# A two-stage kernel with a hand-written order: operand loads and sums moved within a pass, the first step on five banks, low parts and tile copies moved within a step

## The chip, the cores and the metric

The kernel runs on one core of one Trainium2 chip. The metric is the device time of one execution in microseconds (us). Times below are from three unprofiled runs and one profiled execution of the kernel before.

## The reference

Two stages. The first is a complex linear recurrence with an outer-product state, for 4 batches and 8 heads, 768 positions and head size 48; its output y, read as 3072 tokens of width 384, goes into a mixture of 8 experts whose gate P is normalised over rows and columns eight times.

```python
for t in range(S):
    S_re, S_im = a_re*S_re - a_im*S_im + outer(k[t], v[t]), a_re*S_im + a_im*S_re
    y[t] = q[t] @ S_re
x = y as (3072, 384)
P = exp(x @ w_gate - max);  8 times: P /= P.sum(1); P /= P.sum(0); P *= N / E
out = sum over e of P[:, e] * (relu(x @ w1[e]) @ w2[e])      # w1: 384 x 1024, w2: 1024 x 384
```

## The kernel before

Every float32 product is made of three matmuls on two rounded parts (hi x hi, hi x lo, lo x hi), so each operand exists as a high and a low part.

**Phase 1** (about the first 600 us) runs the recurrence in blocks of 256 tokens and, beside it, experts 0 and 1 (`experts`, L193). Their results go by the tile `yst` (L211 to L213) to the tensors ye_d in memory. The Sinkhorn normalisation starts at its end (`phase2a`): `rows` on VectorE, then `columns`, which begins with a small matmul on the sum cs; between them `more(3)` sends three groups of expert work to TensorE (L919 to L930).

**Phase 2** (`phase2b`) runs experts 2 to 7. The tokens are cut into 4 passes (u = 0 to 3) of 768. A pass has 16 steps (m), a step three hidden blocks of 128; I count the steps through, n = 16u + m. Odd passes go through the weights backwards. A step has two kinds of work on TensorE, interleaved by hand:

- 15 products P1 to P15 (`prod`) of sums of weight blocks with sums of token blocks, a scheme of Strassen's kind which takes 15 block products for 18. A product is three matmuls of 384 columns into a PSUM bank. The banks are X and Y, where Z and V take over Y's and P takes over X's. After a product, ACT copies the bank into a tile (`copy`: 11, 12, 21, 31, 32) or VectorE adds it to one (`add`); only then may the next product write the bank. Finished tiles become hh (high part, ACT) and hl (low part, VectorE), the hidden activations; hl00, hl10 and so on name block and token half.
- 18 units (`unit`) of the step before: three matmuls each, from hh and hl into an output bank `po`. When an expert is complete, `finish` (L986) accumulates po, scaled by P, in oa.

`fill(s)`, for slots s = 0 to 14, stands between the products: it issues one or two units, the jobs that `todo` has for this slot, one or two `xjobs`, and a finish. VectorE, ACT and SP take their instructions in this written order. Each is in order, so an instruction that waits holds up all that stand behind it.

Beside this run, by SP's queue: in passes 1 to 3 the weight set of the next step (`load_set`: wa, wb, wc, wd, 768 KB each), in slot 0; in the last step of a pass the 15 operands of the next (`swap`, xP). In passes 1 and 2 the operands of the pass after the next step are made (`forms_late`): eight copies within memory (plain, xf<-x_d), loads of the parts of x (xb, xt), their sums (`full`, L743), and for each form a high part by ACT (stP, L755), a low part by VectorE (L760) and a store (xf). The six y tiles of pass 0 and of the own pass, the results of experts 0 and 1, are loaded by `early` (L961) and added into the result by VectorE (L973); for pass 0 the result is loaded from od, where pass 0 left it, and stored to the output (L975). y, od and stP share the three buffers of the pool `st`.

Of the kernel before, what the change touches and what calls it, by code (L numbers as in the profile page):

```python
# [72 lines left out]
class Net:  # L73
# [122 lines left out]
    def experts(self):  # L196
# [3 lines left out]
        def l2(i, e, f, hh, hl):  # L200
            w2h = self.wt[e, f][:, 0, C:]
            w2l = self.wt[e, f][:, 1, C:]
            for k in range(NCH):
                if f == 0:
                    po[k] = self.psB.tile([128, C], F32, tag="po", name=f"po{e}_{i}_{k}")
                s = slice(k * 128, k * 128 + 128)
                nc.tensor.matmul(po[k], hh[:, s], w2h, start=f == 0, stop=False)  # L207
                nc.tensor.matmul(po[k], hh[:, s], w2l, start=False, stop=False)  # L208
                nc.tensor.matmul(po[k], hl[:, s], w2h, start=False, stop=f == NF - 1)  # L209
                if f == NF - 1:  # L210
                    st = self.xp.tile([128, C], F32, tag="yst", name=f"yst{e}_{i}_{k}")  # L211
                    nc.scalar.activation(st, po[k], AF.Copy)  # L212
                    nc.sync.dma_start(self.ye_d[e][i * NCH + k], st)  # L213
# [677 lines left out]
    def phase2a(self, c2):  # L891
# [30 lines left out]
        for k in range(HEAD):  # L922
            self.rows()
            more(3)
# [9 lines left out]
    def phase2b(self, c2):  # L934
# [89 lines left out]
        xjobs = []  # L1024
        for n, (u, t) in enumerate(steps):
# [21 lines left out]
            if u == 0 and m == 6:  # L1047
                for k in (3, 4, 5, 0, 1, 2):
                    rescale(0, k)
            for uu, ms in ((0, (1, 2, 4, 5, 12, 13)), (u, (6, 7, 8, 9, 10, 11))):  # L1050
                if u and m in ms and (uu or u == 1):
                    y = []
                    todo.setdefault(1, []).append(lambda uu=uu, k=ms.index(m), y=y: y.append(early(uu, k)))
                    todo.setdefault(7, []).append(lambda y=y: y[0]())
# [38 lines left out]
            def fill(s):  # L1093
# [5 lines left out]
                if u and s in (1, 3, 5) and 0 < m < NT - 1 and xjobs:  # L1099
# [3 lines left out]
                if u and m == 0 and s == 14 and xjobs:  # L1103
                    for _ in range(3):
                        xjobs.pop(0)()
                if s < 8 or s in (10, 11, 12):
                    if fin:
                        fin.pop(0)[1]()

            if u and m == 0:  # L1110
                for _ in range(FRONT):
                    unit(*units.pop(0))
            prod("P1", "X", True)
# [44 lines left out]
            l00()  # L1158
# [4 lines left out]
            l10()  # L1163
# [6 lines left out]
            l21()  # L1170
            carry.append(hh(2, 0, c["31"]))
# [184 lines left out]
```

## Time and profile before

| | us |
|---|---|
| median of three runs | 1796.05 (1795.58 to 1797.16) |
| profiled execution | 1798.53 |
| its span, first to last instruction | 1796.8 |
| TensorE busy | 1728.0 |
| VectorE busy | 1270.7 |
| ACT busy | 738.6 |

PE is TensorE's matmul, PEld its weight load, DVE is VectorE, SPq the sequencer that issues transfers. A row of a timeline has the start in us, the duration, the engine, the line, the output and input tiles, and in brackets the idle time ahead of it with what ended it. A row of the list of waits has the total, the count and the longest. Phase 2 begins at 648.2 us of the span; its steps follow each other at about 17 us. A matmul is booked for 0.33 us and starts 0.17 us after the one before, since they are pipelined; the granted clock, PEclk, is 1.00 at full speed.

### The profile page before, as it was taken

The numbers are of one execution on the slowest core, as the hardware profiler recorded it, in microseconds if no ns is written. First come the engines' busy times: TensorE is split into PE (matmuls) and PEld (weight loads), VectorE is DVE, ScalarE is ACT, GpSimd is POOL, SyncE is SP. The second block draws the span as 40 slices with busy tenths as digits, with TensorE's granted clock in tenths as the row PEclk, the third lists the DMA queues.
The fourth block names the chain that finished last, engine by engine and source line by source line (L and its number), as shares of the span: only waits on it lengthen the run. The fifth ranks groups of instructions, "written<-read, shape, count | busy, mean of one in ns | idle before, by whom it ended". The sixth has DMA issues, their size and how long they took to land.

```text
span 1796.8 us, 31293 instructions
## 1 busy us (share of the span) xinstructions
PE 1728.0 (96%) x11774; PEld 1683.8 (94%) x11774; DVE 1270.7 (71%) x2710; ACT 738.6 (41%) x1673; POOL 191.7 (11%) x360
## 2 busy tenths in 40 slices
PE   6989999999999989999997999998999999999998
PEld 4988899999999989999997999997999999999998
DVE  7888999898897668877754566654566655556554
ACT  7544454554544545544522433332433333333231
POOL 3101111111111223334200000000000000000000
PEclk9989999999999999999999999998999999999999
DMA  6434444534357865667558766666666655556550
GB/s 214 115 99 125 109 118 121 155 116 116 110 150 261 324 251 221 255 230 283 203 181 270 254 235 221 231 213 215 228 221 220 222 192 197 200 193 209 191 208 29
DMA packets 160832, 346.04 MB, mean 193 GB/s; under 512 B 15264, under 2 KB 101536, under 8 KB 160672
## 3 DMA queue, kind: packets, MB, share of 16 engines
q1 hardware_dynamic: 155264, 334.03, 54.4%
q0 software_dynamic: 4608, 9.52, 2.2%
q8 instruction: 95, 1.56, 0.3%
q14 instruction: 65, 0.53, 0.1%
q10 hardware_dynamic: 800, 0.39, 0.1%
HBM read 232.53 MB, written 98.70 MB: 184 GB/s over the span
## 4 chain that ended last, share of the span: by engine, by line
PE 79%; DVE 12%; DMA 4%; ACT 2%; issue 2%; SPq 1%; DVEq 0%; ACTq 0%
PE po L1020 10%; PE po L1018 10%; PE po L1019 10%; PE ph L234 8%; PE X L1069 4%; PE X L1071 3%; PE X L1070 3%; PE po L207 3%; PE po L209 3%; PE po L208 3%; PE Y L1069 2%; PE Y L1071 2%; PE Y L1070 2%; PE sp L577 2%; DMA xt<-x_d 2%
## 5 line engine op out<-in xcount | busy, mean ns | idle before, releaser
L1020 PE MATMUL po<-wd,hl 128*128 128x384 f32 x768 | 257.3, 335 | 0.0
L1019 PE MATMUL po<-wd,hh 128*128 128x384 f32 x768 | 257.0, 335 | 0.0
L1018 PE MATMUL po<-wd,hh 128*128 128x384 f32 x768 | 256.9, 335 | 0.0
L234 PE MATMUL ph<-xh,w 128*128 128x256 f32 x1152 | 227.9, 283 | 2.1 <-ACT xh L646 1.2
L234 PEld LDWEIGHTS ph<-xh,w 128*128 128x128 f32 x1152 | 187.1, 191 | 3.1 <-ACT xh L646 1.8
L246 ACT ACTIVATE hh<-ph 128x256 fp32r<-128x256 f32 x192 | 73.3, 382 | 201.2 <-PE ph L234 200.6
L234 PE MATMUL ph<-xl,w 128*128 128x256 f32 x576 | 154.8, 283 | 0.5 <-DVE xl L647 0.5
L1020 PEld LDWEIGHTS po<-wd,hl 128*128 128x128 f32 x768 | 144.4, 188 | 0.8 <-DVE hl L1091 0.2
L1018 PEld LDWEIGHTS po<-wd,hh 128*128 128x128 f32 x768 | 144.5, 188 | 0.0
L1019 PEld LDWEIGHTS po<-wd,hh 128*128 128x128 f32 x768 | 144.5, 188 | 0.0
L207 PE MATMUL po<-w,hh 128*128 128x384 f32 x384 | 140.9, 367 | 2.5 <-ACT yst L212 2.4
L209 PE MATMUL po<-w,hl 128*128 128x384 f32 x384 | 130.7, 340 | 2.6 <-DVE hl L248 2.6
L208 PE MATMUL po<-w,hh 128*128 128x384 f32 x384 | 129.8, 338 | 0.0
L1020 PE MATMUL po<-wc,hl 128*128 128x384 f32 x384 | 128.7, 335 | 0.0
L1018 PE MATMUL po<-wc,hh 128*128 128x384 f32 x384 | 128.7, 335 | 0.0
L1019 PE MATMUL po<-wc,hh 128*128 128x384 f32 x384 | 128.7, 335 | 0.0
L539 POOL DMA_DIRECT2D qs<-z x144 | 77.2, 543 | 444.7 <-ACT hf L247 81.2
L234 PEld LDWEIGHTS ph<-xl,w 128*128 128x128 f32 x576 | 106.5, 190 | 0.9 <-DVE xl L647 0.9
L1090 ACT ACTIVATE hh<-X 128x384 fp32r<-128x384 f32 x64 | 31.5, 492 | 183.4 <-PE X L1071 183.4
L248 DVE TENSOR_TENSOR hl<-hf,hh 128x256 fp32r<-128x256 f32 x192 | 81.7, 427 | 27.6 <-ACT hf L247 26.3
L1001 DVE SCALAR_TENSOR_TENSOR oa<-po,P,oa 128x384 f32<-128x384 f32 x120 | 73.2, 614 | 21.1 <-PE po L1020 20.9
L207 PEld LDWEIGHTS po<-w,hh 128*128 128x128 f32 x384 | 73.1, 190 | 8.0 <-issue 4.0
(1822 smaller groups left out, 4400.2 us busy)
## 6 DMA issues: line engine op xcount, KB each, us to landing
wd<-wd SPq DMA_DIRECT2D x58, 768.0 KB, 6.0
wa<-wd SPq DMA_DIRECT2D x42, 768.0 KB, 4.4
wb<-wd SPq DMA_DIRECT2D x42, 768.0 KB, 5.7
wc<-wd SPq DMA_DIRECT2D x42, 768.0 KB, 4.5
xP<-xf SPq DMA_DIRECT2D x60, 384.0 KB, 4.5
raw<-in_w_dram SPq DMA_DIRECT2D x12, 1152.0 KB, 7.7
wd<-wc SPq DMA_DIRECT2D x16, 768.0 KB, 4.0
wd<-wa SPq DMA_DIRECT2D x16, 768.0 KB, 4.1
```

Of the source, the lines that this page charges most:

```text
L207: nc.tensor.matmul(po[k], hh[:, s], w2h, start=f == 0, stop=False)
L208: nc.tensor.matmul(po[k], hh[:, s], w2l, start=False, stop=False)
L209: nc.tensor.matmul(po[k], hl[:, s], w2h, start=False, stop=f == NF - 1)
L234: nc.tensor.matmul(ph, w[:, k, ct * 128:ct * 128 + 128], x[:, ct, :], start=q == 0, stop=q == len(terms) - 1)
L248: nc.vector.tensor_tensor(hl, hf, hh.bitcast(F32), ALU.subtract)
L539: dma = eng.dma_start(dst[q:q + D - 2:NCT, :, :w], src[:, a, ct * NCH + c, :w])
L1018: nc.tensor.matmul(po[k], hh[:, s], w2[0], start=c == 1, stop=False)
L1019: nc.tensor.matmul(po[k], hh[:, s], w2[1], start=False, stop=False)
L1020: nc.tensor.matmul(po[k], hl[:, s], w2[0], start=False, stop=c == NF)
L1069: nc.tensor.matmul(ps, w[:, 0, k], x[:, 0], start=start, stop=False, skip_group_check=True)
L1070: nc.tensor.matmul(ps, w[:, 0, k], x[:, 1], start=False, stop=False, skip_group_check=True)
L1071: nc.tensor.matmul(ps, w[:, 1, k], x[:, 0], start=False, stop=True, skip_group_check=True)
```

## The change

Seven edits, all in the written order; no instruction is added or dropped.

1. **Loads and sums of the next operands.** In step m = 0 the copies go to slot 4 and the first loads to slots 8 and 9 (all three were in slot 14); in the steps behind it the jobs run in slots 3, 5 and 7 (they were in 1, 3 and 5).
2. **The y tiles** are loaded in slot 2 (before: 1), and summed in slot 1 of the next step (before: slot 7 of the same).
3. **The first step** (n = 0), which has no units between its products, has an order of its own. Z, V and P have banks of their own there, so it uses five banks.
4. **Last low parts:** the add of bank V into 32 stands ahead of hl00, and hl10 behind hl21.
5. **Tile copies:** `finish` may run in slots 9, 10, 11 in place of 10, 11, 12.
6. **yst** of the last block lies in the pool st, which stays, not in the pool of phase 1.
7. **Column sums:** 4, 3 and 2 groups between rows and columns, not 3, 3 and 3.

```diff
-                    st = self.xp.tile([128, C], F32, tag="yst", name=f"yst{e}_{i}_{k}")
+                    if i == self.N // SUB - 1:
+                        st = self.st.tile([128, 2, C], F32R, tag="st", name=f"yst{e}_{i}_{k}").bitcast(F32)[:, 0]
+                    else:
+                        st = self.xp.tile([128, C], F32, tag="yst", name=f"yst{e}_{i}_{k}")
...
-            more(3)
+            more(4 - k)
...
+            todo.setdefault(1, []).extend(late)
+            late = []
             for uu, ms in ((0, (1, 2, 4, 5, 12, 13)), (u, (6, 7, 8, 9, 10, 11))):
                 if u and m in ms and (uu or u == 1):
                     y = []
-                    todo.setdefault(1, []).append(lambda uu=uu, k=ms.index(m), y=y: y.append(early(uu, k)))
-                    todo.setdefault(7, []).append(lambda y=y: y[0]())
+                    todo.setdefault(2, []).append(lambda uu=uu, k=ms.index(m), y=y: y.append(early(uu, k)))
+                    late.append(lambda y=y: y[0]())
...
-                if u and s in (1, 3, 5) and 0 < m < NT - 1 and xjobs:
+                if u and s in (3, 5, 7) and 0 < m < NT - 1 and xjobs:
...
-                if u and m == 0 and s == 14 and xjobs:
-                    for _ in range(3):
-                        xjobs.pop(0)()
-                if s < 8 or s in (10, 11, 12):
-                    if fin:
-                        fin.pop(0)[1]()
+                if u and m == 0 and s in (4, 8, 9) and xjobs:
+                    xjobs.pop(0)()
+                if fin and (s < 8 or s in (9, 10, 11)):
+                    fin.pop(0)[1]()
...
+            if n == 0:
+                prod("P1", "X", True)
+                copy("12", "X")
+                prod("P2", "Y", True)
+                copy("11", "Y")
+                prod("P3", "Z", True)
+                copy("21", "Z")
+                copy("31", "Z")
+                fill(0)
+                prod("P4", "X")
+                add("11", "X")
+                prod("P10", "Y")
+                add("31", "Y")
+                prod("P15", "V", True)
+                copy("32", "V")
+                prod("P7", "X")
+                add("21", "X")
+                prod("P5", "Z")
+                add("11", "Z")
+                l00 = hh(0, 0, c["11"])()
+                prod("P8", "Y")
+                add("32", "Y")
+                prod("P13", "X")
+                add("31", "X")
+                prod("P9", "Y")
+                add("12", "Y")
+                l01 = hh(0, 1, c["12"])()
+                prod("P14", "V")
+                add("31", "V")
+                prod("P11", "X")
+                add("32", "X")
+                l01()
+                l21 = hh(2, 1, c["32"])()
+                prod("P6", "P", True)
+                add("21", "P")
+                l10 = hh(1, 0, c["21"])()
+                prod("P12", "X")
+                hh(1, 1, bank["X"])()()
+                l21()
+                l00()
+                l10()
+                carry.append(hh(2, 0, c["31"]))
+                for k in range(1, 15):
+                    fill(k)
+                continue
...
             add("21", "P")
-            l00()
             l10 = hh(1, 0, c["21"])()
             fill(12)
             prod("P15", "V", True)
             add("32", "V")
-            l10()
+            l00()
             l21 = hh(2, 1, c["32"])()
...
             l21()
+            l10()
```

Three places of the written order, as built. First **SP's queue at the start of pass 1** (step 16 into step 17). od are the stores of pass 0's result, xf2<-x_d2 the eight copies, xb2 and xt2 the loads of x, wa13 to wd13 the next weight set. Before:

```order
L1003 DMA od3_166<-oa_0_9462 128x384
L1003 DMA od4_167<-oa_0_9462 128x384
L1003 DMA od5_168<-oa_0_9462 128x384
L1003 DMA od0_163<-oa_0_9462 128x384
L767 DMA xf2_161<-x_d2_93 128x3x128 x8
L739 DMA xb2_11869<-x_d2_93 128x3x128
L739 DMA xt2_1_12034<-x_d2_93 128x3x128
L739 DMA xb2_11869<-x_d2_93 128x3x128
L739 DMA xt2_2_12037<-x_d2_93 128x3x128
L861 DMA wa13_64_12050<-wd13_156 128x1536
L861 DMA wb13_65_12052<-wd13_156 128x1536
```

Now, from just behind the store od3:

```order
L770 DMA xf2_161<-x_d2_93 128x3x128 x8
L1006 DMA od4_167<-oa_0_9462 128x384
L1006 DMA od5_168<-oa_0_9462 128x384
L742 DMA xb2_11869<-x_d2_93 128x3x128
L742 DMA xt2_1_11969<-x_d2_93 128x3x128
L742 DMA xb2_11869<-x_d2_93 128x3x128
L742 DMA xt2_2_11981<-x_d2_93 128x3x128
L864 DMA wa13_64_12048<-wd13_156 128x1536
L864 DMA wb13_65_12050<-wd13_156 128x1536
L864 DMA wc13_66_12052<-wd13_156 128x1536
L864 DMA wd13_67_12054<-wd13_156 128x1536
L1006 DMA od0_163<-oa_0_9462 128x384
```

The copies stood behind four stores and stand behind one; the loads stand behind three, and the fourth store (od0) behind the weight set.

Second **VectorE at the border of steps 17 and 18**. The names with X, V, P at the end are adds of a bank, hl the low parts, od0<-y0 the sums with y, xb2 and stP1 the work for the next operands. Before:

```order
L1082 TENSOR_TENSOR 21_17_12104<-21_17_12104,P_17_12187 128x384
L1091 SCALAR_TENSOR_TENSOR hl00_17_12182<-11_17_12064,hh00_17_12181 128x384
L1082 TENSOR_TENSOR 32_17_12113<-32_17_12113,V_17_12199 128x384
L1091 SCALAR_TENSOR_TENSOR hl10_17_12194<-21_17_12104,hh10_17_12193 128x384
L1082 TENSOR_TENSOR 31_17_12091<-31_17_12091,V_17_12199 128x384
L1091 SCALAR_TENSOR_TENSOR hl21_17_12206<-32_17_12113,hh21_17_12205 128x384
L760 TENSOR_TENSOR stP1_2_12256<-xt2_3_12096,stP1_2_12256 128x384
L1082 TENSOR_TENSOR 11_18_12245<-11_18_12245,X_18_12224 128x384
L1091 SCALAR_TENSOR_TENSOR hl20_17_12220<-31_17_12091,hh20_17_12219 128x384
L743 TENSOR_TENSOR xb2_11869<-xb2_11869,xt2_4_12098 128x384
L743 TENSOR_TENSOR xb2_11869<-xb2_11869,xt2_5_12118 128x384
L1082 TENSOR_TENSOR 31_18_12271<-31_18_12271,X_18_12224 128x384
```

Now:

```order
L1087 TENSOR_TENSOR 21_17_12099<-21_17_12099,P_17_12184 128x384
L1087 TENSOR_TENSOR 32_17_12108<-32_17_12108,V_17_12195 128x384
L1096 SCALAR_TENSOR_TENSOR hl00_17_12179<-11_17_12062,hh00_17_12178 128x384
L1087 TENSOR_TENSOR 31_17_12089<-31_17_12089,V_17_12195 128x384
L1096 SCALAR_TENSOR_TENSOR hl21_17_12202<-32_17_12108,hh21_17_12201 128x384
L1096 SCALAR_TENSOR_TENSOR hl10_17_12190<-21_17_12099,hh10_17_12189 128x384
L976 SCALAR_TENSOR_TENSOR od0_12082<-y0_12079,P_87,od0_12082 128x384 x2
L1087 TENSOR_TENSOR 11_18_12242<-11_18_12242,X_18_12221 128x384
L1096 SCALAR_TENSOR_TENSOR hl20_17_12217<-31_17_12089,hh20_17_12216 128x384
L763 TENSOR_TENSOR stP1_2_12272<-xt2_3_12113,stP1_2_12272 128x384
L746 TENSOR_TENSOR xb2_11869<-xb2_11869,xt2_4_12115 128x384
L1087 TENSOR_TENSOR 31_18_12267<-31_18_12267,X_18_12221 128x384
```

hl00 and the add of V have changed places, hl10 stands behind hl21, the sums with y have come from inside step 17 to the start of step 18, ahead of its first X add, and the work for the operands (stP1, xb2) stands behind that add.

Third **ACT in step 18 and the queue beside it**, with the semaphores that each row waits for. 11, 31, 21 and 32 are copies of a bank, stP1 the high part of a form; DMAHW0 to 7 are the eight counters which SP's transfers take in turn. ACT before:

```order
L1079 ACTIVATE 11_18_12245<-Y_18_12241 128x384 [waits PE_49,Activation_49]
L1090 ACTIVATE hh20_17_12219<-31_17_12091 128x384 [waits DVE_49]
L755 ACTIVATE stP1_2_12256<-xt2_3_12096 128x384 [waits DMAHW7_49]
L1079 ACTIVATE 31_18_12271<-Y_18_12241 128x384 [waits PE_49,Activation_49]
L1079 ACTIVATE 21_18_12280<-X_18_12224 128x384 [waits PE_49,Activation_49]
```

ACT now:

```order
L1084 ACTIVATE 11_18_12242<-Y_18_12238 128x384 [waits PE_49,Activation_49]
L1095 ACTIVATE hh20_17_12216<-31_17_12089 128x384 [waits DVE_49]
L1084 ACTIVATE 31_18_12267<-Y_18_12238 128x384 [waits PE_49]
L758 ACTIVATE stP1_2_12272<-xt2_3_12113 128x384 [waits DMAHW3_49,DVE_49]
L1084 ACTIVATE 21_18_12279<-X_18_12221 128x384 [waits PE_49,Activation_49]
```

SP now:

```order
L864 DMA wa12_68_12230<-wd12_155 128x1536 [waits DMAHW7_49,PE_49]
L864 DMA wb12_69_12232<-wd12_155 128x1536 [waits DMAHW0_49,PE_49]
L864 DMA wc12_70_12234<-wd12_155 128x1536 [waits DMAHW1_49,PE_49]
L864 DMA wd12_71_12236<-wd12_155 128x1536 [waits DMAHW2_49,PE_49]
L978 DMA out_0_dram<-od0_12082 128x384 [waits DMAHW3_49,DVE_49]
L968 DMA y2_12259<-ye_d0_2_97 128x384 [waits DMAHW4_49]
```

In both the copy to stP1 waits for the store out_0_dram<-od0, whose buffer it takes: the store had counter 7 and was issued in slot 7 of step 17, and has counter 3 now and stands behind the four weight transfers in step 18. The same holds for stP11 and the store of od4 in step 21.

More of the change, by code (lines that the diff above doesn't have):

```diff
@@ L1022, in unit @@
                 fin.append(finish(u, e, k))
-        xjobs = []
+        xjobs, late = [], []
         for n, (u, t) in enumerate(steps):
```

## The prediction

> **What bounds the kernel now.** The page comes first: TensorE is busy nearly all the time, so a change can win only where TensorE waits. The list of TensorE's waits says where.
>
> ```profile
> PE 1728.0 (96%) x11774; PEld 1683.8 (94%) x11774; DVE 1270.7 (71%) x2710; ACT 738.6 (41%) x1673; POOL 191.7 (11%) x360
> ```
> ```profile
> PE X L1069 <- DVE 11_33_14826 L1082: 8.4, 1, 8.4
> PE X L1069 <- DVE 11_17_12064 L1082: 7.3, 1, 7.3
> PE X L1069 <- DVE 32_17_12113 L1082: 2.4, 1, 2.4
> PE X L1069 <- ACT 12_0_8914 L1079: 2.0, 1, 2.0
> PE cp L725 <- DVE cs L721: 1.3, 1, 1.3
> ```
> Two steps stand out, 17 and 33: each is the second step of a pass in which the next pass's operands are prepared. I cut the table by stage at the first matmul of a step (columns: busy time of PE, PEld, DVE, ACT, POOL, then the granted clock, DMA share, GB/s):
>
> ```profile
> 648.16:662.32 14.16, 9.75 (x47) 7.45 (x46) 6.65 (x13) 6.24 (x13) 0.00 (x0) 1.00 0.34 111
> 928.73:945.14 16.41, 15.87 (x91) 15.55 (x91) 9.80 (x19) 5.47 (x11) 0.00 (x0) 1.00 0.21 77
> 945.22:975.02 29.80, 20.02 (x100) 19.06 (x99) 11.88 (x24) 5.47 (x11) 0.00 (x0) 0.89 0.93 304
> 992.40:1009.56 17.16, 17.16 (x100) 17.16 (x100) 8.79 (x18) 8.87 (x18) 0.00 (x0) 1.00 0.60 208
> 1129.77:1147.65 17.88, 17.44 (x100) 17.12 (x100) 13.48 (x27) 5.89 (x12) 0.00 (x0) 1.00 0.67 221
> 1234.83:1262.44 27.61, 19.18 (x101) 18.86 (x100) 10.85 (x22) 5.47 (x11) 0.00 (x0) 0.81 0.93 299
> ```
> Step 19 (992.40) is the undisturbed step: 99 matmuls in 17.16 us, 0.173 each, without a gap. (A window counts a matmul or two of its neighbours.) By it step 17 loses 29.80 - 17.16 = 12.64 us and step 33 27.61 - 17.16 = 10.45. Of this 9.7 and 8.4 are waits; the rest is the lower granted clock behind them (0.89 and 0.81 over the step). Step 0 (648.16) has 45 matmuls, 7.80 us at that rate, and takes 14.16. Step 16 has 90.
>
> VectorE's timeline says what step 17 waits for: a sum for the next pass that stands ahead of the add which TensorE needs.
>
> ```profile
> 945.77 0.61 DVE L1001 SCALAR_TENSOR_TENSOR oa<-po,P,oa 128x384 f32<-128x384 f32 x1
> 954.08 0.56 DVE L743 TENSOR_TENSOR xb<-xb,xt 128x384 f32<-128x384 f32 x1 [7.69 <-DMA xt<-x_d]
> 956.20 0.54 DVE L1082 TENSOR_TENSOR 11_17_12064<-11_17_12064,X 128x384 f32<-128x384 f32 x1
> ```
> SP's timeline says why the load is late: its four stores wait for VectorE one by one, the last until 943.5, and the eight copies and the loads stand behind it. The chain of waits gives the landing.
>
> ```profile
> 933.75 10.09 SPq L1003 DMA_DIRECT2D od<-oa  x4
> 943.89 5.20 SPq L767 DMA_DIRECT2D xf<-x_d  x8
> 949.19 0.56 SPq L739 DMA_DIRECT2D xb<-x_d  x1
> ```
> ```profile
> 949.79 4.19 DMA xt<-x_d
> ```
> **The loads and sums.** In the new order the eight copies follow the first store (933.75), and the loads the third; the fourth store goes behind them. The copies take 5.2 us to issue, so to about 939.5; two stores and four loads of 0.6 us each end at about 943; with 4.2 us to land, the operands are there by 947. The sums move from slot 1 to slot 3 of step 17, behind the add. Slot 3 is eight groups of three matmuls into the step: 945.2 + 8 x 0.52 = 949.4. So 2 us are to spare, and both steps fall to 17.16: **12.64 + 10.45 = 23.1 us gained**. The od load of step 17 also loses its wait for VectorE (the 2.4 us), since its sum now comes a step later.
>
> **The first step.** With five banks the products are further apart from the add that frees their bank. I worked the new order through with the durations of the old step and 0.05 us from an end to what it releases:
>
> ```profile
> 650.83 0.49 ACT L1079 ACTIVATE 12_0_8914<-X 128x384 f32<-128x384 f32 x1 [1.96 <-DMA ye_d<-yst]
> 660.01 0.56 DVE L1082 TENSOR_TENSOR 21_0_8947<-21_0_8947,P 128x384 f32<-128x384 f32 x1
> 660.60 0.52 ACT L1090 ACTIVATE hh<-21_0_8947 128x384 fp32r<-128x384 f32 x1
> ```
> The first copy no longer waits 1.96 us for the store of yst, whose tile has moved to another pool. Three waits remain: P9 for the Y add (0.4 with the restart), P12 for the X add (0.4), and the first product of step 1. It needs bank X, which P12 used last, and ACT has the copy for hh10 ahead of that for hh11: from P6's end 0.56 + 0.52 + 0.49 + 0.55 and four handovers, 2.3 us, of which P12 covers 0.3. So 7.8 + 0.4 + 0.4 + 2.0 = 10.6, **3.6 us gained**. Bounds: 6.4 if nothing waits; 14.16 - 2.0 = 12.2, that is 2.0, if only the yst wait goes.
>
> **The low parts.** An add of bank V now stands ahead of hl00, and the accumulations (oa) of a finished expert one slot earlier. Step 27 shows what that is worth:
>
> ```profile
> 1145.38 0.61 DVE L1001 SCALAR_TENSOR_TENSOR oa<-po,P,oa 128x384 f32<-128x384 f32 x1
> 1145.90 0.54 DVE L1082 TENSOR_TENSOR 32_27_13827<-32_27_13827,V 128x384 f32<-128x384 f32 x1
> ```
> ```profile
> 1146.50 0.44 PE L1069 MATMUL V<-xP,wb 128*128 128x384 f32 x1 [0.44 <-DVE 32_27_13827 L1082]
> ```
> Without the oa (0.53 from start to start) and hl00 (0.47) ahead of it the add ends 1 us earlier, and the wait is gone: 17.88 - 17.16 = 0.72 in each of steps 11, 27, 43, 59, 2.9 together. In steps 16, 32, 48, 90 matmuls x 0.173 = 15.6 against 16.41 in the row above, one group less lies between the two V products, so the add's own 0.55 stays partly open: I take 0.4 of the 0.8, 1.2 together. **4.1 us**, bounds 2.9 and 5.3.
>
> hl10 goes behind hl21, to the start of the next step, 0.47 us ahead of the first X add. In most steps that add waits for TensorE anyhow (2.17 us in the row for step 21); not in steps 9 and 14, where VectorE has no gap:
>
> ```profile
> 894.14 1.02 DVE L879 TENSOR_TENSOR wc<-raw,wc 128x640 fp32r<-128x640 f32 x2
> 895.08 0.61 DVE L1001 SCALAR_TENSOR_TENSOR oa<-po,P,oa 128x384 f32<-128x384 f32 x1
> 895.60 0.54 DVE L1082 TENSOR_TENSOR 11_14_11532<-11_14_11532,X 128x384 f32<-128x384 f32 x1
> ```
> They **lose 0.47 each, 0.9**; after the last step hl10 is late by 0.4. Bounds: 0, and 1.9 if two more such steps appear.
>
> **The column sums.** One group of matmuls moves from the third to the first. Six groups stand in 13.22 us, 2.2 each:
>
> ```profile
> 631.61:644.83 13.22, 13.22 (x94) 13.22 (x95) 11.03 (x28) 4.90 (x13) 6.56 (x12) 1.00 0.97 390
> ```
> ```profile
> 638.60 0.17 DVE L726 TENSOR_SCALAR cs<-cp 128x8 f32<-128x8 f32 x1 [1.12 <-PE cp L725]
> ...
> 643.21 0.52 DVE L721 TENSOR_REDUCE cs<-P 128x8 f32<-128x192 f32 x1
> ```
> The first wait (1.3) goes. But between the second and the third now lie 4.4 us, and VectorE needs from 638.60 to 643.73, 5.1 and 0.3 to begin: a wait of 1.0 comes in. **0.3 gained**, from 1.3 down to a loss of 0.5.
>
> **What comes in.** The sum with y now runs in slot 1 of the next step, and its result is stored just behind that step's weight set. In steps 18 and 21 ACT's copy to stP1 and stP11 writes the buffer that this store reads, and waits for its landing, as it did when the store was issued half a step earlier. Step 21 shows how long a transfer behind wd takes (timeline, then KB and us to landing), and what is due then:
>
> ```profile
> 1026.92 0.32 SPq L861 DMA_DIRECT2D wd<-wd  x1
> 1027.34 1.01 SPq L965 DMA_DIRECT2D y<-ye_d  x2
> ```
> ```profile
> wd<-wd SPq DMA_DIRECT2D x1, 768.0 KB, 5.9
> y<-ye_d SPq DMA_DIRECT2D x2, 192.0 KB, 6.0
> ```
> ```profile
> 1029.60 0.55 DVE L1082 TENSOR_TENSOR 11_21_12760<-11_21_12760,X 128x384 f32<-128x384 f32 x1 [2.17 <-PE X L1071]
> ```
> ```profile
> 1031.67 0.49 ACT L1079 ACTIVATE 21_21_12794<-X 128x384 f32<-128x384 f32 x1 [0.55 <-PE X L1071]
> ```
> ```profile
> 1032.97 0.33 PE L1069 MATMUL X<-xP,wa 128*128 128x384 f32 x1
> ```
> ```profile
> DMA to landing us min/median/max: 2.3/6.4/8.1
> ```
> The two sums fit into VectorE's 2.17 us of idle time, so the store is issued at about 1029.1 and lands behind wd and where y did, at 1033.3. ACT's copy to stP11 follows (0.52, as the hh row above), then the copy 21 that stands behind it, 0.49: 1034.3. P13 needs bank X at 1032.97: 1.3 us and 0.1 of restart, **1.4 lost in each of two steps, 2.8**. Bounds: nothing, if the store lands in the 2.3 us that the quickest store of an stP tile took (last row); 10.2, if it takes the 8.1 of the slowest: 1037.2 + 0.9 - 1033.0 = 5.1, twice. I take the y row, being the same size behind the same wd.
>
> The Trainium skill, "DMA: Bandwidth & Descriptors", sections "Queues, rings and completion order" and "Anatomy of one DMA", says that an engine consumes descriptors in ring order but that completion is not first in, first out per issuing engine, and gives about 2.0 us plus the bytes at 436 GB/s. By it 192 KB would take an estimated 2.5 us, ACT would not be late, and the sum would be the first rival's. The y row (6.0) speaks for the ring order; no row shows a transfer that overtakes.
>
> **The sum.** 23.1 + 3.6 + 4.1 + 0.3 - 0.9 - 0.4 - 2.8 = 27.0 us. The profiled execution took 1798.53 (span 1796.8 and 1.7 around it) and would take 1771.5; it lies 2.5 above the median of the runs, so these would show 1796.05 - 27.0 = 1769.0.
>
> **The rivals.**
>
> 1. The store overtakes the weights and ACT never waits: 27.0 + 2.8, 1766.2. For it: the 2.3 us row. Against: y behind wd.
> 2. The loads are earlier but not early enough: the copies now run where the tail of the operand loads for pass 1 was, and half of the delay stays, 5 us in each of steps 17 and 33: 1779. Against: in step 16 the DMA share was 0.21, the queue was empty and waited for VectorE.
> 3. VectorE takes over: two sums (0.53 each from start to start) and hl10 (0.47) stand ahead of the X add in the 24 steps with y sums. If they found no idle time, each would lose the 1.5 less the 0.7 that the add has to spare (it ends at 1030.15; P7, four groups ahead of P13, comes at 1032.97 - 4 x 0.52 = 1030.9): 24 x 0.8 = 19, so 1788. Against: the 2.17 us. For: steps 9 and 14.
> 4. The queue becomes the bound, and the change is slower. SP issues in order; the od load now waits for the landing of a store behind 3 MB of weights, and the six out stores stand between one weight set and the next. If each of these six held the next set back, TensorE would wait for weights. From 27.0 / 6 = 4.5 us each on the change is slower; at wd's own 5.9 us it is 6 x 5.9 = 35.4, 1804.5. Against: step 21 begins at 1009.6 + 17.16 = 1026.7, and wd is issued 0.2 us later, on TensorE's release, not when the queue is free; the queue has most of a step to spare.
> 5. The move does nothing for steps 17 and 33, because the sums meet another late transfer in slot 3: 1796.05 - 27.0 + 23.1 = 1792. Against: nothing else is waited for there in the timeline.
>
> **How the numbers follow.** The forecast has 0.67, the rivals 0.15, 0.06, 0.06, 0.03 and 0.03. The likeliest time is 1769.0. Downwards the bounds of the first step, the low parts and the store add 2.8 + 1.2 + 2.8, not all together: 1763. Upwards a first step at its lower bound, a store at 8.1 us in one step, and two more full VectorE steps add 1.6 + 3.7 + 1.0, and half of rival 2 lies there: 1776. Rivals 3, 4 and 5 and the rest of 2 are left out, some 0.15. About 0.2%, 3.6 us, is what a measurement can tell from no change. Faster by more than that: all but rival 4 and part of 5, 0.95; within it 0.02; slower 0.03.
>
> **What would show it.** In the new profile: step 17 and step 33 at about 17.2 with a granted clock of 1.00, no wait of VectorE for xt there, and SP's x8 copies right behind the first od store; step 0 at 10 to 11 us with its longest wait ahead of the first product of step 1; no wait of a V product in steps 11, 27, 43, 59; in steps 18 and 21 an ACT stP that waits for DMA, then 1.4 us of TensorE for copy 21; a wait for cs at the third column sum. A wait of TensorE for a weight tile, or more than 1 us lost in the steps with y sums, would prove me wrong; step 17 still above 20 us would take away most of the sum.

## The result and the profile after

| | before | after |
|---|---|---|
| median of the runs, us | 1796.61 (1795.58 to 1797.35) | 1778.24 (1775.23 to 1779.53) |
| profiled execution, us | 1798.53 | 1778.05 |
| its span, us | 1796.8 | 1776.2 |
| ratio of the times | 1 | 0.9896, 95% interval 0.9879 to 0.9913 |

The kernel is faster by 18.4 us, 1.0%. The forecast was 27.0 us and 1769.0, with a range that ended at 1776. The sign and most terms of the sum came out; the term for step 18 did not. Medians and ratios, here and below, leave out the one execution in the slow state, 4352.33 us in the variant with the y tiles as before.

The busy time of the page after the change, and its list of TensorE's waits (total, count, longest). The lines shown stand 3 to 5 lines later than in the old kernel; L1069 is L1074:

```profile
PE 1722.9 (97%) x11774; PEld 1681.9 (95%) x11774; DVE 1270.7 (72%) x2710; ACT 738.4 (42%) x1673; POOL 190.7 (11%) x360
```
```profile
PE X L1074 <- ACT 21_18_12279 L1084: 7.3, 1, 7.3
...
PE X L1074 <- DVE hl L1096: 1.7, 1, 1.7
PE X L1074 <- ACT 21_21_12792 L1084: 1.5, 1, 1.5
...
PE po L1023 <- DVE hl L1096: 1.0, 3, 0.4
```

The waits for VectorE in steps 17 and 33 (7.3, 2.4 and 8.4) are gone. A wait for ACT in step 18 has come, as long as the one in step 17 was. The table by stage, cut at the first matmul of steps 0, 9, 16, 17, 18, 21, 22, 27 and 33 (columns as in the table of before):

```profile
645.46:655.98 10.52, 8.54 (x46) 7.58 (x45) 6.35 (x13) 6.01 (x13) 0.00 (x0) 1.00 0.23 88
799.22:816.89 17.67, 17.45 (x100) 17.13 (x100) 13.64 (x26) 8.37 (x17) 6.22 (x12) 1.00 0.64 245
922.61:938.63 16.02, 15.90 (x91) 15.58 (x91) 8.94 (x17) 5.46 (x11) 0.00 (x0) 1.00 0.64 191
938.63:955.79 17.16, 17.16 (x100) 17.16 (x100) 11.36 (x23) 5.46 (x11) 0.00 (x0) 1.00 0.84 286
955.79:982.22 26.43, 19.15 (x101) 18.84 (x101) 10.95 (x22) 5.76 (x12) 0.00 (x0) 0.87 0.66 243
...
1016.54:1035.52 18.98, 17.43 (x100) 17.11 (x100) 10.48 (x21) 5.76 (x12) 0.00 (x0) 1.00 0.63 228
1035.52:1053.39 17.87, 17.47 (x100) 17.11 (x100) 13.22 (x26) 5.88 (x12) 0.00 (x0) 1.00 0.68 231
1122.03:1139.19 17.16, 17.16 (x100) 17.16 (x100) 13.61 (x27) 5.88 (x12) 0.00 (x0) 1.00 0.66 230
1226.07:1243.23 17.16, 17.16 (x100) 17.16 (x100) 11.38 (x23) 5.46 (x11) 0.00 (x0) 1.00 1.03 360
```

Steps 17, 33 and 27 now have no gap. Step 18 takes 26.43, of which 7.3 is the wait and the rest of the loss the lower clock behind it (0.87). SP's timeline shows how this came about:

```profile
937.72 0.61 SPq L864 DMA_DIRECT2D wa<-wd  x1
...
939.37 0.43 SPq L864 DMA_DIRECT2D wd<-wd  x1
940.33 1.31 SPq L1006 DMA_DIRECT2D od<-oa  x2
941.69 1.10 SPq L968 DMA_DIRECT2D y<-ye_d  x2
951.79 0.32 SPq L971 DMA_DIRECT2D od<-od  x1
...
955.59 0.56 SPq L864 DMA_DIRECT2D wa<-wd  x1
...
957.19 0.62 SPq L864 DMA_DIRECT2D wd<-wd  x1
958.17 1.09 SPq L978 DMA_DIRECT2D out_dram<-od  x1
```

And SP's own waits between 938 and 956 us, the time from issue to landing of the out store (KB, us), and ACT's timeline:

```profile
SPq L971 <- DMA od<-oa: 8.9, 1, 8.9
```
```profile
out_dram<-od SPq DMA_DIRECT2D x1, 192.0 KB, 10.3
```
```profile
968.52 0.52 ACT L758 ACTIVATE stP<-xt 128x384 fp32r<-128x384 f32 x1 [8.40 <-DMA out_dram<-od]
968.95 0.47 ACT L1084 ACTIVATE 21_18_12279<-X 128x384 f32<-128x384 f32 x1
```

To be seen here: the weight set of step 18 is issued at 937.7. Behind it stands the store of output tile 0 (od0), whose accumulation the fifth edit moved out of step 16. The od load reads what that store writes, so SP stands for 8.9 us, until 951.79. The operand loads and the next weight set, which had nothing to wait for, go out only then, the set in one burst at 955.6 to 957.2. The out store behind it lands at 958.17 + 10.3 = 968.5. Only then may ACT write stP1 into the buffer, and the copy of 21 behind it frees bank X at 969.4.

Compared step by step, before to after, the spans differ by 20.6 us, made up so (gains first): steps 17 and 33 23.2; step 0 3.6; the V products (steps 11, 27, 43, 59 and 16, 32, 48) 4.2; the column sums 1.1; steps 28 and 34, of which nothing was forecast, 0.7; 1.6 in phase 1 ahead of anything that was changed, which is from run to run (that part ended between 597.2 and 603.4 us in the traces of this case). Lost: step 18 9.1, step 21 1.8, steps 22 and 30 1.2, steps 9 and 14 1.0, the end 0.8.

### The profile page after: what moved, and what is told of

Same layout as the page of the kernel before. It is cut to its first block, busy times and chain, and to the rows that moved or that the text cites. A ratio compares the mean times of both kernels' runs of the same rounds, so it can differ in the third digit from the quotient of the medians.

```text
span 1776.2 us, 31227 instructions
## 1 busy us (share of the span) xinstructions
PE 1722.9 (97%) x11774; PEld 1681.9 (95%) x11774; DVE 1270.7 (72%) x2710; ACT 738.4 (42%) x1673; POOL 190.7 (11%) x360
## 4 chain that ended last, share of the span: by engine, by line
PE 82%; DVE 11%; DMA 3%; ACT 2%; issue 2%; SPq 1%; DVEq 0%; ACTq 0%
PE po L1023 11%; PE po L1021 11%; PE po L1022 11%; PE ph L237 8%; PE X L1074 4%; PE X L1076 4%; PE X L1075 4%; PE po L207 3%; PE po L209 3%; PE po L208 3%; PE Y L1074 2%; PE Y L1076 2%; PE Y L1075 2%; PE sp L580 2%; PE y L597 2%
```

## The experiments

All but one are edits of the changed kernel. The ratio is to the kernel before, run again beside each group of variants. The times of the steps come from the one profile of each variant, and they carry the argument: medians of different groups can differ by a few us, as phase 1 alone does. The set's begin and the landing of the out store are counted in us from the start of step 18 (the set is that of step 19).

| run | step 17 | step 18 | step 21 | set begins | store lands | median us | ratio to before |
|---|---|---|---|---|---|---|---|
| changed kernel | 17.16 | 26.43 | 18.99 | -0.20 | 12.64 | 1778.24 | 0.9896 [0.9879, 0.9913] |
| four buffers | 17.16 | 17.16 | 17.16 | -1.20 | 12.14 | 1767.86 | 0.9823 [0.9784, 0.9863] |
| od0 early | 17.16 | 23.40 | 19.50 | -1.98 | 9.92 | 1774.11 | 0.9856 [0.9822, 0.9891] |
| copies last | 17.16 | 22.47 | 17.16 | -5.53 | 8.81 | 1772.45 | 0.9862 [0.9840, 0.9884] |
| copies last, od0 early | 17.16 | 18.76 | 17.16 | -5.53 | 6.68 | 1771.13 | 0.9860 [0.9844, 0.9877] |
| store on POOL | 17.16 | 24.23 | 21.80 | -0.05 | 9.39 | 1778.58 | 0.9892 [0.9877, 0.9907] |
| set on POOL | 18.18 | 23.27 | 21.07 | -5.26 | 9.64 | 1778.59 | 0.9892 [0.9875, 0.9908] |
| y as before | 23.43 | 17.16 | 17.16 | | | 1774.69 (three) | 0.9865 [0.9821, 0.9909] |
| operands alone | 23.98 | 17.16 | 17.16 | | | 1781.19 | 0.9906 [0.9890, 0.9921] |
| hl10 as before | 17.16 | 26.14 | 19.01 | -1.34 | 12.18 | 1777.23 | 0.9876 [0.9842, 0.9911] |
| yst, columns as before | 17.16 | 25.21 | 18.99 | -2.09 | 10.62 | 1780.85 | one run |
| four buffers, order | 17.16 | 17.16 | 17.16 | -2.00 | 11.23 | 1764.13 | 0.9813 [0.9799, 0.9826] |

In three kernels in which nothing bears on step 18 it took 26.43, 26.14 and 25.21; a difference of about 1 us there is from run to run.

### Four buffers

```diff
-        self.st = c2.enter_context(tc.tile_pool(name="st", bufs=3, side="right"))
+        self.st = c2.enter_context(tc.tile_pool(name="st", bufs=4, side="right"))
-        ctp = c2.enter_context(tc.tile_pool(name="ct", bufs=9))
+        ctp = c2.enter_context(tc.tile_pool(name="ct", bufs=8))
```

> The pool st has four buffers (before: three), the pool of tiles c eight (before: nine, of which at most six are in use at a time). Theory 1 and its rival agree that TensorE waits in steps 18 and 21 only since ACT's copy to stP1 and stP11 takes the buffer that the out store still reads. With a fourth buffer the tile is another one, ACT doesn't wait, and both steps fall to 17.2: 9.3 + 1.8 = 11 us, about 1767. SP's 8.9 us at the od load stay and cost nothing. Rival 3 (the late weight set is itself the bound, and ACT's wait only comes first): step 18 or 19 now waits for a weight tile, and less than 5 us are gained.

Steps 18 and 21 in the table by stage, and ACT's stP1 in step 18:

```profile
956.20:973.36 17.16, 17.16 (x101) 17.16 (x101) 10.96 (x22) 5.89 (x12) 0.00 (x0) 1.00 0.99 360
1007.68:1024.84 17.16, 17.16 (x101) 17.16 (x101) 10.48 (x21) 5.89 (x12) 0.00 (x0) 1.00 0.72 252
```
```profile
960.48 0.52 ACT L758 ACTIVATE stP<-xt 128x384 fp32r<-128x384 f32 x1
```

Both losses are gone, although the out store lands as late as before (12.14) and the od load goes out as late (951.52 here). So the shared buffer is the way by which a late store reaches TensorE, and the late weight set costs nothing by itself. Rival 3 falls. What made the store late in step 18 is a question of its own.

### Output tile 0 early

```diff
-                if fin and (s < 8 or s in (9, 10, 11)):
+                if fin and (s < 8 or s in (9, 10, 11) or n == NT and s == 12):
```

> Only one thing differs from the changed kernel: the accumulation of output tile 0 of pass 0 and its store to od run in slot 12 of step 16, ahead of step 18's weight set in SP's queue, and no longer at the start of step 17 behind it. Theory 1 (the block): step 18 takes 26.4 us because the od load in step 17 waits 8.9 us for the landing of a store behind 3 MB of weights; SP stands still, the next weight set is issued in one burst at 955.6 to 957.2, and the out store behind it lands only at 968.4, so that ACT's copy to stP1 is late. Then the 8.9 us of SP go, the set is issued about 6 us earlier, and step 18 falls to what step 21 shows, about 19.0 (17.16 + 1.8); the kernel gains some 7 us on the changed one, about 1771. Step 16 may lose up to 0.4 (one accumulation ahead of the V add). Rival 2 (the transfers themselves are too many in steps 17 and 18: eight copies within memory, two sets, loads and stores): the out store lands at about the same time, step 18 stays above 25 us and the time at about 1778.

Step 18 came between the two, at 23.40. The long wait for od0 is gone from SP's list (937 to 953 us, total, count, longest), but four others stand there now:

```profile
SPq L742 <- DMA wc<-wd: 2.6, 1, 2.6
SPq L971 <- DMA wa<-wd: 1.9, 1, 1.9
SPq L742 <- DMA wb<-wd: 1.6, 1, 1.6
SPq L742 <- DMA wd<-wd: 1.3, 1, 1.3
```

The od load and three operand loads wait for the four weight transfers, with which they share no data. Each is the eighth transfer behind the one it waits for. The program itself asks for this: SP's transfers take eight counters in turn, and each first waits for its own counter, which the eighth transfer ahead of it used (DMAHW in SP's rows of the written order). In the trace of the changed kernel 764 of SP's 800 transfers have such a wait in front of them. None of the 800 starts before the eighth ahead of it has landed (the nearest 0.016 us after it), while 44 start before the seventh has. So eight can be under way, and a set of four takes half of these places for as long as it is. So the block by od0 was one part, 2 to 3 us of step 18, and the set of step 18 itself another.

### Copies last, and both

In the operand jobs of passes 1 and 2 an empty job stands where the eight copies were, and the copies are the last:

```diff
-        jobs = [plain, load(*B12), ...
+        jobs = [plain if u < 2 else lambda: None, load(*B12), ...
-        return jobs
+        return jobs + [plain] * (u >= 2)
```

> The changed kernel, with the eight copies within memory (xf<-x_d) as the last of a pass's operand jobs and not in slot 4 of its first step; the loads and sums keep their slots. Theory 4 (backlog): in the changed kernel the DMA engines are full from 928 to 968 us, and what fills them first are the eight copies, about 9 us of it; the set of step 18 is issued only behind them, 4 to 5 us later than a set usually is, SP's queue is held by it, and the set of step 19 and the out store are late in turn. Without the copies there the set of step 18 is issued about 4 us ahead of step 17, od0's store lands behind it at about 946 and not 951.7, the set of step 19 goes out when its tiles are free, and step 18 falls to what step 21 shows, about 19: 7 us less, about 1771. Rival: the two sets and the eleven other transfers of step 17 fill the engines by themselves, and step 18 stays above 23 us. A step late in the pass may pay for the copies there.

The set of step 18 now goes out at 932.6, 5.9 us ahead of step 17, and the od load is free at 946.5, as expected; the next set begins 5.53 us ahead of step 18, as in most steps. Yet step 18 is at 22.47, again between the two. SP's timeline and step 18:

```profile
932.59 0.61 SPq L864 DMA_DIRECT2D wa<-wd  x1
...
946.46 0.32 SPq L971 DMA_DIRECT2D od<-od  x1
...
950.15 0.35 SPq L864 DMA_DIRECT2D wa<-wd  x1
```
```profile
955.68:978.15 22.47, 19.02 (x100) 18.70 (x100) 10.95 (x22) 5.76 (x12) 0.00 (x0) 0.92 0.60 213
```

The operand loads behind the od load still went out at 947.3 to 949.8, just ahead of the set, and the set landed 2 us later than in step 21 (8.27 after the step's start, there 6.27).

> As the run with the copies last, and with output tile 0 of pass 0 accumulated and stored in slot 12 of step 16, ahead of the set. If the backlog is what decides, the store of od0 no longer matters, and step 18 is as in that run within 0.5 us, about 19. If the block of SP by od0's store and the backlog add, step 18 is another 3 us shorter (as it was from 26.4 to 23.4), that is 17.2, or it was not at 19 before.

```profile
952.04:970.80 18.76, 17.45 (x101) 17.13 (x100) 10.96 (x22) 5.77 (x12) 0.00 (x0) 1.00 0.66 240
```

18.76, and the store lands 6.68 after the start, as in step 21 of the changed kernel (6.84). The two add, within the 1 us from run to run: 4.0 us for the copies alone, 3.0 for od0 alone, 7.7 of the 9.3 for both; the 1.6 that stay are much like step 21's 1.8. Step 21 itself is at 17.16 in both runs, since the list of jobs is one longer and in that step stP11 now stands behind the copies of 21 and 32 in ACT's order. In step 18 stP1 stands where it stood, so there the gain is not from this shift.

### The out store, and the weight sets, on another queue

```diff
-                    nc.sync.dma_start(self.out[tt * CH:tt * CH + CH, :], r)
+                    nc.gpsimd.dma_start(self.out[tt * CH:tt * CH + CH, :], r)
```

> The changed kernel, with the six out stores of the y sums issued on POOL's queue, which has nothing else to send at that time; SP's queue keeps the rest. If a store lands late since it stands behind the weight set in the same queue (ring order), it now lands 2 to 3 us after its issue, ACT's stP1 and stP11 find their buffer free at about 961 of step 18 and in step 21, and both steps fall to 17.2 to 17.7: some 10 us gained on the changed kernel, about 1768, though SP still stands 8.9 us at the od load. Rival: the 16 DMA engines take what has been issued first, whatever its queue; then the store still lands with wd (968 and 1023), step 18 stays above 25 us and step 21 at 19.0.

KB and us to landing, first for step 18, then for step 21:

```profile
wd<-wd SPq DMA_DIRECT2D x1, 768.0 KB, 11.1
...
out_dram<-od POOLq DMA_DIRECT2D x1, 192.0 KB, 6.7
```
```profile
wd<-wd SPq DMA_DIRECT2D x1, 768.0 KB, 6.2
...
out_dram<-od POOLq DMA_DIRECT2D x1, 192.0 KB, 5.5
```

On an empty queue the store still takes 6.7 and 5.5 us. In step 18 it lands at 958.34 + 6.7 = 965.0, ahead of wd (957.24 + 11.1 = 968.3); in step 21 at 1016.89 + 5.5 = 1022.4, behind wd (1014.44 + 6.2 = 1020.6). The order within the queue, by which the forecast reasoned, is thus not the whole cause: on another queue too the store is slow while the weights are under way. How much of this is POOL's own path, no run separates; the six out stores took 3.3 to 6.7 us there and 3.7 to 10.3 on SP's queue. The Trainium skill, "DMA: Bandwidth & Descriptors", section "Queues, rings and completion order", says that each DMA engine takes turns between the queues it has work for, packet by packet. Step 18, where the store overtakes wc and wd, agrees with that; step 21 does not show it.

In the next run the line of `load_set` is changed in the same way.

> The changed kernel, with the weight sets of passes 1 to 3 issued on POOL's queue; SP's keeps the stores, the y, od and operand loads. In the traces so far no transfer on SP's queue starts before the eighth one ahead of it has landed, so a set of four holds half of the places. Theory 1b (SP's queue holds the set up): in step 17 the od load and the four operand loads no longer stand behind the set, and the set of step 19 is issued when its tiles are free, about 6 us before step 18 and not at 955.6 to 957.2; the out store then has less ahead of it and step 18 falls from 26.4 to what step 21 shows, 19 to 20; about 1771 if POOL's own issue costs nothing elsewhere. Rival (the 16 DMA engines are full with the two sets, whatever the queue): step 18 stays above 23 us. In both cases step 21 stays at 19 to 22, as in the run with the out stores on POOL's queue. A wait of TensorE for a weight tile in any step would be a cost of POOL's queue.

It hardly tells the two apart: 23.27 is just above the 23 at which the rival was to hold. The set began 5.26 us ahead of step 18, as theory 1b wanted, but took longer (wb below; 7.6 in the changed kernel, where it was issued in a burst), and the store landed at 9.64:

```profile
wb<-wd POOLq DMA_DIRECT2D x1, 768.0 KB, 8.5
```

Steps 17 and 33 got longer too (18.18 and 21.03), so the move to POOL's queue has a price of its own.

### The parts of the change by themselves

The kernel before, with the first edit alone:

```diff
-                if u and s in (1, 3, 5) and 0 < m < NT - 1 and xjobs:
+                if u and s in (3, 5, 7) and 0 < m < NT - 1 and xjobs:
...
-                if u and m == 0 and s == 14 and xjobs:
-                    for _ in range(3):
-                        xjobs.pop(0)()
+                if u and m == 0 and s in (4, 8, 9) and xjobs:
+                    xjobs.pop(0)()
```

> The kernel before with the first edit alone: copies, loads and sums of the next operands in the new slots, all else as before. If the first edit carries the gain by itself, steps 17 and 33 both fall to 17.2: 23.1 us, about 1773. The run with the y tiles loaded and summed as before (step 17 at 23.4) says otherwise for step 17: there the sum in slot 7 waits for the od load, which lands behind the weight set. Then step 33, which has no od load, falls to 17.2 and step 17 to about 23.4: 10.4 + 6.5 = 17 us, about 1779; and steps 18 and 21 stay at 17.2 to 17.4, since the out store of the sum is then issued half a step earlier.

Steps 17 and 33:

```profile
944.75:968.73 23.98, 19.84 (x100) 19.52 (x100) 11.94 (x24) 5.47 (x11) 0.00 (x0) 0.86 0.85 298
...
1227.82:1244.98 17.16, 17.16 (x100) 17.16 (x100) 10.86 (x22) 5.47 (x11) 0.00 (x0) 1.00 1.01 358
```

The second expectation holds: 10.4 in step 33 and only 5.9 in step 17. The rest of step 17 needs the later sum. The same is seen from the other side when the second edit is taken back in the changed kernel:

```diff
-            todo.setdefault(1, []).extend(late)
-            late = []
...
-                    todo.setdefault(2, []).append(lambda uu=uu, k=ms.index(m), y=y: y.append(early(uu, k)))
-                    late.append(lambda y=y: y[0]())
+                    todo.setdefault(1, []).append(lambda uu=uu, k=ms.index(m), y=y: y.append(early(uu, k)))
+                    todo.setdefault(7, []).append(lambda y=y: y[0]())
```

> The y tiles are loaded in slot 1 and summed in slot 7 of the same step again, as in the kernel before; all else is as in the changed kernel. Theory 1: steps 18, 21, 22 and 30 return to 17.2, 9.3 + 1.8 + 1.2 = 12.3 us gained; but in step 17 VectorE's sum now waits for the od load, which waits for the store behind the weight set (landing at 951.7, so the sum ends at about 955), and the X add behind it is late: step 17 takes about 24 to 26 us, and some 4 us are left, about 1774. Rival (the sum in the next step is free, and step 18's loss comes from the operand loads alone): step 18 stays above 25 us.

VectorE in step 17 (the sum with od, and the add behind it), and step 17:

```profile
951.55 1.27 DVE L976 SCALAR_TENSOR_TENSOR od<-y,P,od 128x384 f32<-128x384 f32 x2 [5.48 <-DMA od<-od]
952.74 0.55 DVE L1087 TENSOR_TENSOR 32_17_12108<-32_17_12108,X 128x384 f32<-128x384 f32 x1
```
```profile
937.52:960.95 23.43, 19.21 (x100) 18.50 (x100) 12.46 (x25) 5.47 (x11) 0.00 (x0) 0.93 0.88 310
```

The sum's delay by the od load is 5.5 us, and step 17 loses 6.3. Two other steps are longer than in the changed kernel: step 20 with 18.35 and step 28 with 17.70 (17.16 each there). Steps 18, 21 and 22 are back at 17.2, step 30 only to 17.61. So the second edit buys 8.0 us, 6.3 of it in step 17, and gives 12 back.

The low part hl10 ahead of the V add again:

```diff
             l00()
+            l10()
             l21 = hh(2, 1, c["32"])()
...
             l21()
-            l10()
```

> The low part hl10 is taken ahead of hl21 and of the add of bank V into 31 again, as in the kernel before; all else is as in the changed kernel. If the low part at the step's start is what makes steps 9, 14 (0.48 and 0.47), 22, 30 (0.6 each) and the last (0.4 of 0.8) longer, then 9 and 14 return to 17.2 and 17.9, the end loses 0.4, and 22 and 30 lose most of their 0.6: 2 to 2.6 us, about 1776; V products still don't wait in steps 11, 27, 43, 59, since the low part stands behind the add that frees the bank. If V's wait comes back there (0.7 each, and 0.4 in steps 16, 32, 48), then it was hl10 and not hl00 that the wait hung on, and the time is about 1780. Steps 18 and 21 stay as they are.

Step 9 is at 17.19 and step 14 at 17.87, as before the change; step 27 stays at 17.16, so V's wait hung on hl00 and the accumulation, as forecast. But steps 22 and 30 stay at 17.87 and 17.84 (step 22 below), so hl10 is not their cause:

```profile
1033.91:1051.77 17.86, 17.46 (x100) 17.10 (x100) 13.22 (x26) 5.88 (x12) 0.00 (x0) 1.00 0.70 230
```

yst and the column sums as before (their two hunks of the change's diff undone):

> The changed kernel with yst in the pool of phase 1 and three groups of expert work ahead of each column sum, as in the kernel before. Step 0 gets the wait of its first copy for the store of yst back: 10.5 + 2.0 = 12.5 us. The column sums: from the first to the third (VectorE's read of cp) 12.4 us as before, where the changed kernel has 10.9. My forecast gave this edit 0.3 us, the trace of the changed kernel shows 1.1 between the last group and phase 2; if the 1.1 is the edit's and not a change from run to run, it is lost here again.

Step 0, and the 4 us in step 1 behind it:

```profile
646.53:658.81 12.28, 8.84 (x47) 7.56 (x46) 6.37 (x13) 5.92 (x13) 0.00 (x0) 1.00 0.38 128
660.00:664.00 4.00, 4.00 (x17) 4.00 (x16) 2.65 (x6) 2.59 (x6) 0.00 (x0) 0.60 0.56 230
```

The wait costs 1.8 us in step 0, and 1.55 more in step 1 (19.44 against 17.89), which ran at a granted clock of 0.60 for 4 us: together 3.3 in this trace, where 2.0 was reckoned. The fall of the clock does not come each time: in the kernel before, with the yst wait too, step 1 took 17.76. For the column sums, the stretch from VectorE's first test of fl to the first product of phase 2, here and in the changed kernel:

```profile
601.20:646.53 45.33, 44.08 (x309) 43.40 (x307) 29.70 (x79) 22.97 (x58) 20.84 (x36) 1.00 0.91 357
```
```profile
601.27:645.46 44.19, 44.05 (x308) 43.36 (x307) 29.15 (x79) 22.73 (x58) 20.92 (x36) 1.00 0.98 381
```

The edit is worth 1.1 us here. In the other kernels with the edit the same stretch is 44.2 to 44.8, and in the two without it 45.3, so the worth is 0.5 to 1.1.

### A version of its own

Four buffers, hl10 as before, and the y sums in slot 2 of the next step:

```diff
-            todo.setdefault(1, []).extend(late)
+            todo.setdefault(2, []).extend(late)
```

> The changed kernel with four buffers in the pool st (and eight of nine c tiles), hl10 as in the kernel before, and the y sums in slot 2 of the next step, behind the low part hl20 and the first X add, in place of slot 1. If the parts add up: steps 18 and 21 at 17.2 (as in the run with four buffers), 9 and 14 shorter by 0.48 each, the end by 0.4 (as in the run with hl10 as before), and, if the y sums ahead of hl20 are what makes steps 22 and 30 wait for hl, these fall by 0.6 each: 11.1 + 1.0 + 0.4 + 1.2 = 13.7 us below the changed kernel, about 1764.5. Rival: steps 22 and 30 stay at 17.85, then hl20 is late for another reason. If a store issued 1 us later now comes too late for another tile of the pool, a step of pass 1 gets longer by 1 us or more.

Steps 22 and 30:

```profile
1021.58:1038.82 17.24, 17.24 (x101) 17.08 (x100) 13.10 (x26) 5.88 (x12) 0.00 (x0) 1.00 0.74 238
1158.94:1176.18 17.24, 17.24 (x101) 17.08 (x101) 13.11 (x26) 5.47 (x11) 0.00 (x0) 1.00 0.36 127
```

The parts add up: 1764.13 us where 1764.5 was expected, 1.9% below the kernel before (0.9799 to 0.9826) and, by the medians of two groups, 14 us below the changed one. Steps 22 and 30 lost their 0.6 because the y sums stood ahead of hl20.

## Why the prediction was right and wrong, point by point

**What failed** is the part "What comes in": 1.4 us in each of steps 18 and 21. Its mechanism was right in both (the store behind the set, ACT's wait in front of copy 21, TensorE's wait for X). The term that was mis-sized is the time to landing of step 18's store. In step 21 the loss measured 1.8, and the store took 1023.38 - 1018.92 = 4.5 us from issue to landing. In step 18 it measured 9.3 against 17.16. The time to landing had been read from step 21, where the set lies spread over 6 us and ends 6.3 us after the step's start, and carried over to step 18, which was never looked at. There the set came late and in a burst, and the store took 10.3 us; the upper bound, 8.1 us, was the slowest stP store and too low. In the kernel before, where these two stores go out half a step earlier, they took 2.0 and 1.8 us. It is the second edit that puts the store behind the next set: with it undone step 18 is at 17.16. How late the store then is, the three runs on od0 and the copies show by two causes that add: the eight copies ahead of step 18's weight set, and od0's store, which the fifth edit put behind that set. The copies stood ahead of this set in the old kernel too; there the out store went out ahead of the next set, and so did it in the two runs with the y tiles as before, in which step 18 took 17.16.

**Rival 4** had named the thing ("the od load now waits for the landing of a store behind 3 MB of weights") and was given 0.03, on a count over all six stores and on step 21 as the counter-evidence. It struck in one step, by way of a late store and not of missing weights. The forecast had followed the od load only as far as VectorE, where it indeed no longer waits (step 17 is at 17.16), and not SP, which waits in VectorE's place; that every instruction behind it then goes out 9 us later was not worked out.

**Rival 1** (the store overtakes the weights) does not hold on SP's queue: the store landed 0.5 and 0.6 us behind wd. The estimate of 2.5 us beside the forecast uses a figure that the Trainium skill, "DMA: Bandwidth & Descriptors", section "Anatomy of one DMA", gives for GpSimd's path, and the store stood on SP's. **Rival 2** (half of the delay stays in steps 17 and 33) has nearly the measured total, 1779, but by luck: nothing of the delay stays there, so it is refuted. **Rival 3** (VectorE takes over) shows in steps 22 and 30 alone, 0.6 each, and not by the X add but by hl20, which these steps need early. **Rival 5** falls with rival 2.

**Loads and sums:** 23.1 forecast, 23.2 measured; step 17 needs the first and the second edit together, step 33 the first alone, and the forecast had credited it all to the first, but for the od wait of 2.4. **First step:** 3.6 and 3.6; it takes 10.52 where 10.6 was worked out, with the longest wait ahead of step 1's first product (1.7) as said. In the one trace without the move of yst the clock made the loss 1.3 us larger than reckoned. **Low parts and tile copies:** 4.1 and 4.2. **Steps 9 and 14:** 0.9 and 1.0, and undone when hl10 goes back. **The end:** 0.4 and 0.8; it is 34.4 with hl10 back and 34.2 to 34.6 in most other variants, against 34.0 before, so what takes it is open. **Column sums:** 0.3 forecast, 0.5 to 1.1 measured; the sign was right, but the wait of 1.0 that was to come at the third sum is 0.14 to 0.75 in the traces with the edit.

In sum: of the 8.6 us between forecast and medians (27.0 and 18.4) the steps of the two traces explain 8.2. Step 18 makes 7.7, counted from its 17.38 before; steps 22 and 30 1.2, step 21 and the end 0.4 each, and the column sums and steps 28 and 34 give 1.5 back.

## What to carry to other kernels

When a transfer's time to landing is taken from one place of the trace, look up what is in flight at the place where it will be used; a store of 192 KB took 4.5 us in one step and 10.3 in another of the same kernel. When an edit takes a wait from a compute engine, follow the queue that waits in its place to everything behind it. One more buffer between the late store and the next writer took away the whole loss of steps 18 and 21 (11.1 us in the traces); the two ways of making the store earlier together left 1.6 of it (9.5 gained, of which step 21's 1.8 came with the shift of stP11). By the medians, 10.4 and 7.1, the two are not told apart for certain: the intervals of their ratios overlap.

## What the runs showed of the hardware

SP never had more than eight transfers under way: in every trace none of its 632 to 800 transfers started before the eighth ahead of it had landed. The eight counters of the program ask for this, so whether the chip's queue takes more is not shown. A load can thus wait for weights with which it has nothing in common, 1.3 to 2.6 us each in the run with od0 early.

The time to landing of the same 192 KB store differed with what was under way: 2.0 us in the kernel before and 10.3 in the changed one for the store of step 18, 1.8 and 4.5 for that of step 21. On a queue of its own it took 6.7 and 5.5. A queue of its own is thus no sure way past the weights.

TensorE's clock did not follow the length of a wait alone. In phase 2 each wait from 2.9 to 8.4 us was followed by 8 to 17 matmuls at 0.32 us in place of 0.17. Of the shorter waits some were and some were not: 2.1 us in step 21 was with the sets on POOL's queue and was not with od0 early, and the same wait of 2.0 us in step 0 was in the run with the operands alone and not in the kernel before. In the traces' records the granted clock then stood at 0.50 for 3.41, 6.83 or 10.24 us (the last fall, which the kernel's end cuts off, aside). The Trainium skill, "TensorE: Matmul & The Clock Gate", section "Part 1: The HAM clock gate", says that the clock falls after at least one idle window of about 3.4 us, and that the window runs freely. The multiples of 3.41 us and the chance agree with windows that run freely; the falls after waits of 2.0 to 2.9 us do not agree with a whole idle window.
